# A top-k attention with a feed-forward behind it: the feed-forward's matmuls placed by the parity of the slot from the first block on

## The chip, the cores and the metric

The kernel runs on one core of one Trainium2 chip. The metric is the device time in microseconds (us); the kernel before took 1437.44 us as the median of three runs (1435.94 to 1437.99).

## The reference

Attention over 8 batches, 8 heads, 576 positions and a head size of 64, in float32. Each row of scores keeps its 32 largest values and drops the rest, then softmax, then the values. The result, 4608 tokens by 512, goes through a feed-forward whose activation is `h * cos(h)`:

```python
scores = scale * np.matmul(q, k.transpose(0, 1, 3, 2))
kth = np.partition(scores, -top_k, axis=-1)[..., -top_k:-top_k + 1]
scores = np.where(scores >= kth, scores, -1000000000.0)
attn = np.exp(scores - np.max(scores, axis=-1, keepdims=True))
attn = attn / (np.sum(attn, axis=-1, keepdims=True) + 1e-09)
x = np.matmul(attn, v).transpose(0, 2, 1, 3).reshape(B * S, H * D)
h = x @ w_in            # 512 -> 2048
out = (h * np.cos(h)) @ w_out   # 2048 -> 512
```

## The kernel before

**Units, slots, blocks.** A unit is 128 tokens for one pair of heads. There are 36 tiles of 128 tokens and 4 pairs, so 144 units, numbered 0 to 143. The main loop has one slot for each unit. In slot i, VectorE (DVE) searches the 32 largest scores of unit i (`topk_first`, `topk_round`), ScalarE (ACT) masks and exponentiates unit i-1 (`mask`, `exponentials`), GpSimd (POOL) splits unit i-2 into halves that go to DRAM and come back transposed (`split`, `write_halves`, `transposes`), and TensorE (PE) computes the scores of units ahead (`scores`) and, in even slots, the values of two units behind (`values`), which DVE scales into `xT` (`take_values`, L473). The four units of one tile make a block of the feed-forward. A tile that crosses from one batch to the next has two parts, so its matmuls are cut smaller.

**The search.** DVE folds each row of 576 scores into 288 maxima (`fold_high`, L260) and 288 minima. The minima come from POOL as sum minus maximum (`fold_sum` L276, `fold_low` L285), or, for the units in `BUSY` (7 to 10), from DVE (`fold_now`, L268).

**The feed-forward, in items.** PE's part of a block is 16 items: eight of `ff1` (256 of the 2048 hidden columns, L522), written here as a0 to a7, and eight of `ff2` (two of the 16 accumulation steps of the output, L597), written as B0, B2, ... B14 by their first step. Two items of `ff1` fill one PSUM bank. `take_first` (ACT, L536 and L538) empties the bank; after two banks the block has a tile of 1024 columns, on which POOL runs `reduce_first` (L558) and `reduce_second` (L567), ACT the sine (`sines`, L577) and POOL the product (`gate`, L584). After the last slot, `ff["end"]` moves the reductions and the gate to DVE. The feed-forward has two PSUM banks: one is held by the `ff2` of a block from its first item to its last, the other serves the `ff1` items two at a time.

**What sets the order.** The engines' orders are written out by hand: each engine executes its instructions in the order of the Python calls. `slot` (L696) calls `feed` three times: after round 2 of the search and before the scores and values, after round 3, and at its end. `feed(n)` places up to n items, taking turns between the two kinds (`kind`, `half`), as long as there is credit; credit grows by 5.0 in a slot less 0.9 for each unit scored there, up to 5.3 (L790). `can_first` asks that the block's `xT` is complete for two calls of `feed` and that a tile is free; `can_second` that the gate was placed at least `lag` calls ago (2, and 3 in the middle of the kernel, L627). After the last slot, `drain` runs three times and then `forward` until nothing is left, each placing two items.

**The weights.** Both matrices (w_in and w_out) arrive as 64-bit words in 32 chunks of 512 KB (`load_weights`) and are decoded during the first slots in three steps: ACT (`decode_first`, L133, L136), DVE (`decode_second`, L144), POOL (`decode_third`, L154). Twelve slots (`decoding`) are treated specially: there the sines and a gate come early in the slot (L710 to L712), and `ff["late"]` is false, so that reductions need not wait for the next slot.

Of the kernel before, what the change touches and what calls it, by code (L numbers as in the profile page):

```python
# [30 lines left out]
def kernel(  # L31
# [16 lines left out]
    NP = H // 2  # L48
# [43 lines left out]
        w_out.append(w)  # L92
        chunks.append((moe_w_out[f * P : (f + 1) * P, :], w))
    CHUNKS, XB = 7, 3
    BUSY = range(7, 11)
    ff = {"live": 0, "tick": 0, "now": 0, "credit": 0.0, "end": False, "kind": 0, "half": 0, "open": 0, "late": False}

    wq = {"next": 0, "loaded": deque(), "second": deque(), "third": deque(), "done": 0, "ready": 0}

    def staged(spare=0):  # L100
        return sum(c[2] == spare for k in ("loaded", "second", "third") for c in wq[k])
# [70 lines left out]
    NU = len(units)  # L172
# [81 lines left out]
    def fold_high(u):  # L254

        s, sc = u["s"], u["sc"]
        if u["n"] not in BUSY:
            del u["sc"]
# [13 lines left out]
    def fold_sum(u):  # L272

        s = u["s"].bitcast(I32)
        u["low"] = work.tile([P, 2, HS], F32, tag="low", name="low", bufs=1)
        nc.gpsimd.tensor_tensor(  # L276
            out=u["low"].bitcast(I32), in0=s[:, :, 0:HS], in1=s[:, :, HS:S], op=ALU.add
        )

    def fold_low(u):  # L280

        if u["n"] in BUSY:
            return
# [19 lines left out]
    def topk_first(u, w):  # L303

        u["top"] = tops[u["n"] % len(tops)]
        if w:
            merge_first(w)
        if u["n"] not in BUSY:
            fold_sum(u)
        fold_high(u)  # L310
        if w:
            merge_second(w)
        if u["n"] in BUSY:
            fold_now(u)
# [22 lines left out]
    def merge_first(u):  # L337
        n = TOPK // 2 + 1
        u["lesser"] = u["top"].rearrange("p j r i -> p j (r i)")[:, :, 2 * n : 3 * n]
        nc.vector.tensor_reduce(  # L340
            out=u["lesser"], in_=u["top"][:, :, 0:n], axis=mybir.AxisListType.X, op=ALU.min
        )
# [138 lines left out]
    for w in widths:  # L481
# [9 lines left out]
    first = deque((blk, i) for blk in blocks for i in range(2 * NF * blk["w"] // 512))  # L491
    second = deque(
        (blk, i, f) for blk in blocks for i in range(blk["w"] // P) for f in range(0, NF, 2)
    )
# [11 lines left out]
    def ff1(blk, i):  # L506
        w = blk["w"]
        nf = 256 // w
        part = i % 4
        if part == 0:  # L510
            blk["g"].append(ffw.tile([P, 1024], F32, tag="g", name="g", bufs=CHUNKS))
            blk["x"] = ffw.tile([P, 1024], F32, tag="x", name="x", bufs=XB)
            ff["live"] += 1
        if part % 2 == 0:
            open_bank()
            blk["mm"] = ps.tile([P, 512], F32, tag="mm", name="mm", bufs=2)
        g, mm = blk["g"][-1], blk["mm"]
        for a in range(nf):
            f = i * nf + a
            at = (part % 2 * nf + a) * w  # L520
            for c in range(NC):
                nc.tensor.matmul(  # L522
                    mm[:, at : at + w],
                    w_in[f // FC][:, c, (f % FC) * P : (f % FC + 1) * P],
                    blk["xT"][:, c],
                    start=c == 0,
                    stop=c == NC - 1,
                )
        if part % 2 == 0:
            return  # L530
        ff["open"] -= 1
        full.append((take_first, blk, g, blk["x"], mm, part // 2))
# [37 lines left out]
    def sines(least):  # L570

        n = sum(c[3] < ff["now"] for c in waiting)
        if n == 0 or (n < least and waiting[0][3] + 2 > ff["now"]):
            return
        for _ in range(n):
            blk, g, x, _ = waiting.popleft()
            nc.scalar.activation(out=x, in_=x, func=AF.Sin, bias=halfpi, scale=TWO_PI_BELOW)  # L577
            sined.append((blk, g, x))

    def gate(n):  # L580
        for _ in range(min(n, len(sined))):
            blk, g, x = sined.popleft()
            eng = nc.vector if ff["end"] else nc.gpsimd
            eng.tensor_tensor(out=g, in0=g, in1=x, op=ALU.mult)  # L584
            blk["gated"].append(ff["tick"])

    def ff2(blk, i, f0):
        w = blk["w"]
        if f0 == 0:
            open_bank()  # L590
            blk["o"] = ps.tile([P, 512], F32, tag="mm", name="o2", bufs=2)
        o = blk["o"]
        per = 1024 // w
        for f in range(f0, f0 + 2):
            g = blk["g"][f // per]
            at = (f % per) * w + i * P
            nc.tensor.matmul(  # L597
                o, g[:, at : at + P], w_out[f], start=f == 0, stop=f == NF - 1
            )
        if f0 + 2 < NF:  # L600
            return
        ff["open"] -= 1
        full.append((take_second, blk, i, o))
# [10 lines left out]
    def can_first():  # L614
        if not first:
            return False
        blk, i = first[0]
        if blk["left"] or ff["tick"] < blk["tick"] + 2 or wq["ready"] < (((i + 1) * (256 // blk["w"]) - 1) // FC + 1) * NC:
            return False
        return i % 4 > 0 or ff["live"] + staged() < CHUNKS  # L620

    def can_second():
        if not second:
            return False
        blk, i, f = second[0]

        lag = 3 if 3 * NP < ff["now"] < NU - NP else 2  # L627
        gated = sum(ff["tick"] >= t + lag for t in blk["gated"])
        return gated * 1024 // blk["w"] >= f + 2 and wq["ready"] >= NC * NF // FC + f + 2

    def feed(n):

        ff["tick"] += 1
        while n > 0 and ff["credit"] >= 1:
            kinds = (ff["kind"], 1 - ff["kind"])
            if ff["end"] and second and second[0][2] == 0:
                kinds = (0, 1)
            for kind in kinds:
                if (can_first, can_second)[kind]():
                    break  # L640
            else:
                return
            if kind == 0:
                ff1(*first.popleft())
            else:
                ff2(*second.popleft())
            if kind != ff["kind"] or ff["half"]:
                ff["kind"], ff["half"] = 1 - kind, 0
            else:
                ff["half"] = 1  # L650
            n, ff["credit"] = n - 1, ff["credit"] - 1

    scored, last, last_values = {}, {}, {}  # L660
    for i, u in enumerate(units):
# [13 lines left out]
    for n in range(NP, len(order)):  # L675
        i = last[order[n - 6]] if n >= 6 else 0
        load_at(max(i, 2 * NP + 2), load_qk, *order[n])
        i = last_values[order[n - 6]] if n >= 6 else 0
# [15 lines left out]
        transposes(x)  # L694

    def slot(i, u, w, x, z):  # L696
        n = (3, 4, 4, 3, 4, 3)[i] if i < NP + 2 else 2
        if i < NP:
            for load, b, hp in at_once[i]:
                load(b, hp)  # L700
        load_weights(n, nc.sync if i < NP + 2 else nc.scalar)
        if x:
            (turn if i < NP + 2 else send)(x)
        decoding = i < 3 * NP
        ff["late"] = False
        topk_first(u, w)
        fold_low(u)
        topk_round(u, 1)
        topk_round(u, 2)
        if decoding:  # L710
            sines(1)
            gate(1)  # L712
        decode_second(NP)
        decode_third()
        reduce_first()
        reduce_second()
        made = scored.get(i, [])
        if z:
            take_banks()
        feed(1)  # L720

        for m in made:
            scores(m)
        if z:
            values(z)


        if i % 2 and not decoding:
            sines(1)
        if w:  # L730
            mask(w)
        take_banks()
        if w:
            exponentials(w)
        if i + 1 < NU:
            take_scores(units[i + 1])
        topk_round(u, 3, both(w), z)
        ff["late"] = not decoding
        if i in at_slot:
            load, b, hp = at_slot[i]  # L740
            load(b, hp)
        gate(1)
        feed(1 if len(made) == 2 else 2)
        take_banks()
        decode_first(NP)
        reduce_first()
        reduce_second()
        feed(1 if len(made) == 2 else 3)

    def forward(n):  # L750
        ff["now"] += 1
        ff["credit"] = n
        take_banks()
        gate(2)
        reduce_first()
        reduce_second()
        sines(1)
        gate(2)
        feed(n)

    def drain(w, x, z):

# [24 lines left out]
    take_scores(units[0])  # L787
    decode_first(3)
    for i in range(NU):
        ff["credit"] = min(ff["credit"] + 5.0 - 0.9 * len(scored.get(i, [])), 5.3)  # L790
        ff["now"] += 1
        wq["ready"] = wq["done"]
        u, w, x = (units[i - n] if n <= i else None for n in range(3))
        z = units[i - 4 : i - 2] if i % 2 == 0 and i >= 4 else None
        if NP < i < NP + 3:
            z = units[2:4] if i == NP + 1 else None
        slot(i, u, w, x, z)
# [44 lines left out]
```

## Time and profile before

| | |
|---|---|
| median of 3 runs | 1437.44 us |
| the profiled execution: its own time | 1436.91 us |
| its span (first to last instruction) | 1435.1 us |
| PE busy | 1378.2 us, 96% |
| DVE busy | 1356.7 us, 95% |
| POOL, ACT busy | 1161.1 us, 1093.1 us |
| mean granted PE clock | 0.977 |

Times inside the profile are counted from the first instruction. Lines such as L597 are those of the listing above. "PEld" is PE's loading of weights, which overlaps its matmuls. The name of a group reads output <- inputs. Every matmul of the code appears as two in the trace, so an item of `ff1` is 16 of them and an item of `ff2` is 4.

### The profile page before, as it was taken

Reading aid. Unit: us, or ns where it says so; the run is one execution under the profiler, and the core shown is the slowest. Engines: PE = TensorE matmul, PEld = TensorE weight load, DVE = VectorE, ACT = ScalarE, POOL = GpSimd, SP = SyncE. Lnnn points to the kernel's source line nnn. Section 1 sums busy time; section 2 is a strip of 40 time slices with the busy share of each in tenths; the row PEclk is TensorE's granted clock in tenths of the full one; section 3 lists DMA queues with packets and bytes.
Section 4 is the critical chain, followed back from the end, with each engine's and each line's share of the span. In section 5 each row is a group of like instructions: output and inputs, shape, how many; then the busy total and the mean of one; then the engine's idle time right before and its main releaser. Section 6 shows DMA issues by size and latency. Waiting matters only on the chain.

```text
span 1435.1 us, 30310 instructions
## 1 busy us (share of the span) xinstructions
PE 1378.2 (96%) x10304; PEld 982.1 (68%) x10304; DVE 1356.7 (95%) x5236; ACT 1093.1 (76%) x1922; POOL 1161.1 (81%) x810
## 2 busy tenths in 40 slices
PE   5678899999999999999999999999999999999998
PEld 3455567777777767777777777777777777777765
DVE  8989999999999999999999999999999999999931
ACT  7877787787777787777778787777787778777742
POOL 5786888888888888888888898888888888888810
PEclk7698999999999999999999999999999999999999
DMA  9466676566655576557655557656755566655540
GB/s 306 175 183 176 191 202 182 142 172 190 180 161 152 152 190 185 162 147 202 181 158 151 155 170 196 179 140 178 192 173 155 155 159 165 172 147 146 153 100 15
DMA packets 427436, 240.01 MB, mean 167 GB/s; under 512 B 375952, under 2 KB 392592, under 8 KB 427280
## 3 DMA queue, kind: packets, MB, share of 16 engines
q1 hardware_dynamic: 420720, 224.22, 57.3%
q10 hardware_dynamic: 6560, 13.85, 2.7%
q8 instruction: 81, 1.33, 0.4%
q14 instruction: 75, 0.61, 0.1%
HBM read 45.09 MB, written 101.19 MB: 102 GB/s over the span
## 4 chain that ended last, share of the span: by engine, by line
PE 88%; DVE 10%; POOL 1%; ACT 1%; issue 0%; POOLq 0%; ACTq 0%
PE o L597 34%; PE mm L522 33%; PE rim L465 11%; PE sc L238 8%; DVE top L352 4%; DVE rest L357 3%; PE rim L238 2%; DVE low L357 1%; DVE rest L260 1%; DVE w_in L144 0%; POOL w_out L154 0%; POOL halves L412 0%; DVE w_out L144 0%; PE warm L782 0%; DVE xT L473 0%
## 5 line engine op out<-in xcount | busy, mean ns | idle before, releaser
L522 PEld LDWEIGHTS mm<-xT,w_in 128*128 128x128 f32 x4608 | 537.0, 192 | 72.2 <-issue 65.0
L597 PE MATMUL o<-w_out,g 128*128 128x512 f32 x1152 | 542.5, 606 | 18.3 <-POOL g L584 18.0
L522 PE MATMUL mm<-xT,w_in 128*128 128x128 f32 x4608 | 539.4, 276 | 4.6 <-DVE xT L473 3.0
L352 DVE MAX8 top<-rest 128x8 f32<-128x288 f32 x1152 | 478.8, 451 | 0.0
L412 POOL COPY halves<-s 128x2304 uint16<-128x2304 uint16 x140 | 294.6, 2104 | 151.4 <-ACT s L389 146.0
L357 DVE MATCH_REPLACE8 rest<-top,rest 128x288 f32<-128x288 f32 x864 | 376.4, 443 | 0.0
L597 PEld LDWEIGHTS o<-w_out,g 128*128 128x128 f32 x1152 | 205.3, 193 | 210.1 <-issue 190.5
L352 DVE MAX8 top<-low 128x8 f32<-128x288 f32 x576 | 241.7, 448 | 0.0
L389 ACT ACTIVATE s<-s,nd 128x576 f32<-128x576 f32 x288 | 220.1, 766 | 0.8
L285 POOL TENSOR_TENSOR low<-low,rest 128x576 int32<-128x576 int32 x140 | 197.7, 1412 | 11.0
L381 ACT ACTIVATE s<-s,top 128x576 f32<-128x576 f32 x288 | 206.1, 766 | 0.0
L276 POOL TENSOR_TENSOR low<-s 128x576 int32<-128x576 int32 x140 | 197.4, 1410 | 4.7 <-ACT s L252 4.7
L536 ACT ACTIVATE g<-mm 128x512 f32<-128x512 f32 x144 | 85.9, 597 | 140.7 <-PE mm L522 140.0
L567 POOL TENSOR_TENSOR x<-g,x 128x1024 f32<-128x1024 f32 x68 | 161.4, 2373 | 5.7
L584 POOL TENSOR_TENSOR g<-g,x 128x1024 f32<-128x1024 f32 x68 | 160.8, 2364 | 2.2 <-ACT x L577 2.2
L238 PE MATMUL sc<-k,q 64*128 64x448 f32 (+1 forms) x640 | 147.1, 580 | 6.2 <-DVE top L352 5.4
L465 PE MATMUL rim<-pT,v 128*64 128x128 f32 (+1 forms) x2560 | 146.2, 268 | 0.0
L465 PEld LDWEIGHTS rim<-pT,v 128*64 128x64 f32 x2560 | 128.3, 138 | 12.4 <-issue 11.1
L248 ACT COPY s<-sc 128x896 f32<-128x896 f32 x144 | 127.8, 888 | 3.2 <-PE sc L238 3.2
L252 ACT COPY s<-rim 128x256 f32<-128x256 f32 (+1 forms) x160 | 59.1, 369 | 90.3 <-PE rim L465 90.1
L357 DVE MATCH_REPLACE8 low<-top,low 128x288 f32<-128x288 f32 x288 | 125.4, 443 | 0.0
L260 DVE TENSOR_TENSOR rest<-sc,s 128x576 f32<-128x576 f32 x144 | 107.7, 748 | 6.4 <-ACT s L252 6.0
(55 smaller groups left out, 1210.9 us busy)
## 6 DMA issues: line engine op xcount, KB each, us to landing
rows<-halves SPq DMA_DIRECT2D x140, 640.0 KB, 3.0
out_dram<-ob ACTq DMA_DIRECT2D x36, 256.0 KB, 2.0
q<-in_q_dram SPq DMA_DIRECT2D x31, 288.0 KB, 3.4
st<-in_moe_w_in_dram SPq DMA_DIRECT2D x16, 512.0 KB, 6.8
v<-in_v_dram SPq DMA_DIRECT2D x32, 256.0 KB, 3.2
k<-in_k_dram SPq DMA_DIRECT2D x31, 144.0 KB, 3.3
k<-in_k_dram SPq DMA_DIRECT2D x32, 128.0 KB, 3.6
st<-in_moe_w_out_dram SPq DMA_DIRECT2D x8, 512.0 KB, 4.9
```

The costliest lines, as they stand in the source:

```text
L238: nc.tensor.matmul(to[r0 : r0 + rows, rim_bank(r0, j) if k0 else place(u["hp"], j), 0 : k1 - k0], st["q"][d, q0 : q0 + rows], st["k"][d, k ...
L276: nc.gpsimd.tensor_tensor(out=u["low"].bitcast(I32), in0=s[:, :, 0:HS], in1=s[:, :, HS:S], op=ALU.add)
L285: nc.gpsimd.tensor_tensor(out=low, in0=low, in1=u["rest"][:, :, HS:S].bitcast(I32), op=ALU.subtract)
L352: nc.vector.max(to[:, j], src[:, j])
L357: nc.vector.match_replace(rest[:, j], to[:, j], src[:, j], NEG)
L381: nc.scalar.activation(out=s[:, j], in_=s[:, j], func=AF.Prelu, bias=less[:, j, 1:2], scale=1.0, alpha=FAR)
L389: nc.scalar.activation(out=s[:, j], in_=s[:, j], func=AF.Exp, bias=nd[:, j : j + 1], scale=SCALE, accum_out=den[:, j, 0:1],)
L412: nc.gpsimd.tensor_copy(out=halves[:, :, 0 : 2 * S], in_=s.rearrange("p (k h) -> p h k", h=2))
L465: nc.tensor.matmul(room[i][d, r], lhsT, rhs, start=c == NT, stop=c == NT - 1)
L522: nc.tensor.matmul(mm[:, at : at + w], w_in[f // FC][:, c, (f % FC) * P : (f % FC + 1) * P], blk["xT"][:, c], start=c == 0, stop=c == NC - 1,)
L567: nc.gpsimd.tensor_tensor(out=x, in0=g, in1=x, op=ALU.subtract)
L597: nc.tensor.matmul(o, g[:, at : at + P], w_out[f], start=f == 0, stop=f == NF - 1)
```

## The change

`feed` no longer takes turns and counts no credit. It gets a list of kinds (0 for `ff1`, 1 for `ff2`) and places one item of each kind in the list if the gates allow it. Odd slots ask for a, then B B, then a a; even slots for B, then B, then a. `can_first` refuses before slot 6. The lag of 3 holds from the start, except near the end. `ff["late"]` is true in the decode slots as well, whose sines move to the place that they have later and whose early gate is dropped. Slot 3 loads four weight chunks and not three. `BUSY` loses unit 7. After the last slot, `feed_any` keeps the taking of turns, without credit, and the rule that a first `ff2` item lets `ff1` go ahead no longer asks for `ff["end"]`.

```diff
-    BUSY = range(7, 11)
+    BUSY = range(8, 11)
...
-        return i % 4 > 0 or ff["live"] + staged() < CHUNKS
+        return ff["now"] > NP + 2 and (i % 4 > 0 or ff["live"] + staged() < CHUNKS)
...
-        lag = 3 if 3 * NP < ff["now"] < NU - NP else 2
+        lag = 3 if ff["now"] < NU - NP else 2
...
-    def feed(n):
+    def item(kind):
+        if not (can_first, can_second)[kind]():
+            return False
+        if kind == 0:
+            ff1(*first.popleft())
+        else:
+            ff2(*second.popleft())
+        return True
+
+    def feed(*kinds):
 
         ff["tick"] += 1
-        while n > 0 and ff["credit"] >= 1:
+        for kind in kinds:
+            item(kind)
+
+    def feed_any(n):
+
+        ff["tick"] += 1
+        for _ in range(n):
             kinds = (ff["kind"], 1 - ff["kind"])
-            if ff["end"] and second and second[0][2] == 0:
+            if second and second[0][2] == 0:
                 kinds = (0, 1)
-            for kind in kinds:
-                if (can_first, can_second)[kind]():
-                    break
+            if item(kinds[0]):
+                kind = kinds[0]
+            elif item(kinds[1]):
+                kind = kinds[1]
             else:
                 return
-            if kind == 0:
-                ff1(*first.popleft())
-            else:
-                ff2(*second.popleft())
             if kind != ff["kind"] or ff["half"]:
                 ff["kind"], ff["half"] = 1 - kind, 0
             else:
                 ff["half"] = 1
-            n, ff["credit"] = n - 1, ff["credit"] - 1
...
-        n = (3, 4, 4, 3, 4, 3)[i] if i < NP + 2 else 2
+        n = (3, 4, 4, 4, 4, 3)[i] if i < NP + 2 else 2
...
-        if decoding:
-            sines(1)
-            gate(1)
...
-        feed(1)
+        feed(0 if i % 2 else 1)
...
-        if i % 2 and not decoding:
+        if i % 2 or decoding:
             sines(1)
...
-        ff["late"] = not decoding
+        ff["late"] = True
...
-        feed(1 if len(made) == 2 else 2)
+        feed(*((1, 1) if i % 2 else (1,)))
...
-        feed(1 if len(made) == 2 else 3)
+        feed(*((0, 0) if i % 2 else (0,)))
...
     def forward(n):
...
-        ff["credit"] = n
...
-        feed(n)
+        feed_any(n)
...
-        ff["credit"] = min(ff["credit"] + 5.0 - 0.9 * len(scored.get(i, [])), 5.3)
```

More of the change, by code (lines that the diff above doesn't have):

```diff
@@ L94 @@
     CHUNKS, XB = 7, 3
-    BUSY = range(7, 11)
-    ff = {"live": 0, "tick": 0, "now": 0, "credit": 0.0, "end": False, "kind": 0, "half": 0, "open": 0, "late": False}
+    BUSY = range(8, 11)
+    ff = {"live": 0, "tick": 0, "now": 0, "end": False, "kind": 0, "half": 0, "open": 0, "late": False}
     wq = {"next": 0, "loaded": deque(), "second": deque(), "third": deque(), "done": 0, "ready": 0}
```

## The prediction

> **What bounds the kernel now.** I read the page first: busy shares, slices, the chain that ended last.
>
> ```profile
> PE 1378.2 (96%) x10304; PEld 982.1 (68%) x10304; DVE 1356.7 (95%) x5236; ACT 1093.1 (76%) x1922; POOL 1161.1 (81%) x810
> ...
> PE   5678899999999999999999999999999999999998
> ...
> PEclk7698999999999999999999999999999999999999
> ...
> PE 88%; DVE 10%; POOL 1%; ACT 1%; issue 0%; POOLq 0%; ACTq 0%
> ```
>
> PE is idle for 57 us of the span, nearly all in the first six slices, where its clock is also cut. After that it is full. So the end comes at the moment from which PE runs without a gap, plus its remaining work, plus gaps at the end. The waits of the middle (230 to 1340 us) say the same: PE waits for nothing, and DVE only a little for the values that PE makes.
>
> ```profile
> DVE xT L473 <- ACT s L252: 11.8, 57, 0.6
> ```
>
> From the starts of the fold (L260), which opens a slot on DVE, two slots take 18.64 us when PE is full; where DVE sets the pace (slots 12 to 17) they take 18.38, an even one 9.39 and an odd one 8.99. PE's own sum for two slots is the same 18.64: four `ff1` items at 1.79, four `ff2` items at 1.72 to 1.82, scores 2.15, values 2.28. Then the timeline of the start, PE, DVE and POOL.
>
> ```profile
> 76.64 5.62 PE L522 MATMUL mm<-xT,w_in 128*128 128x128 f32 x48
> 88.74 6.34 PE L597 MATMUL o<-w_out,g 128*128 128x512 f32 x8 [6.47 <-POOL g L584]
> ...
> 112.35 8.19 PE L597 MATMUL o<-w_out,g 128*128 128x512 f32 x12 [7.63 <-POOL g L584]
> ...
> 151.54 3.26 PE L597 MATMUL o<-w_out,g 128*128 128x512 f32 x4 [3.93 <-POOL g L584]
> ```
> ```profile
> 85.96 3.01 DVE L144 TENSOR_SCALAR w_out<-w_out 128x512 int32<-128x512 int32 x2
> ...
> 105.18 0.49 DVE L473 TENSOR_TENSOR xT<-rim,pT 128x128 f32<-128x128 f32 x2 [3.62 <-ACT s L252]
> ```
> ```profile
> 86.17 2.51 POOL L584 TENSOR_TENSOR g<-g,x 128x1024 f32<-128x1024 f32 x1
> ```
>
> PE stands in front of an `ff2` item whose gate is still on POOL, three times, with scores and values queued behind it. The first time, DVE pays 3.62 us for it in slot 8. Each time PE then runs at half clock (eight matmuls in 6.34 us, against 3.44 later). And in slot 7 two decode steps of DVE take 3.01 us instead of 0.67, over the same stretch as POOL's gate.
>
> Last, the end, PE and ACT.
>
> ```profile
> 1363.70 1.88 PE L597 MATMUL o<-w_out,g 128*128 128x512 f32 x4
> 1365.42 1.95 PE L522 MATMUL mm<-xT,w_in 128*128 128x128 f32 x16
> 1367.21 3.60 PE L597 MATMUL o<-w_out,g 128*128 128x512 f32 x8
> 1370.64 1.95 PE L522 MATMUL mm<-xT,w_in 128*128 128x128 f32 x16
> 1373.85 2.05 PE L522 MATMUL mm<-xT,w_in 128*128 128x128 f32 x16 [1.26 <-ACT x L538]
> ```
> ```profile
> 1369.48 0.20 ACT L379 ACTIVATE nd<-nd 128x2 f32<-128x2 f32 x1 [1.46 <-DVE nd L372]
> ...
> 1371.68 0.76 ACT L389 ACTIVATE s<-s,nd 128x576 f32<-128x576 f32 x1
> 1372.34 0.19 ACT L389 ACTIVATION_READ_ACCUMULATOR s<-s,nd 128x1 f32 x1
> 1372.63 0.60 ACT L536 ACTIVATE g<-mm 128x512 f32<-128x512 f32 x1
> ```
>
> An `ff1` pair waits until ACT has emptied the bank of the pair before it, and that emptying stands behind the last unit's exponentials. Here it costs PE 1.26 us, because two `ff2` items (3.44 us) and a lone `ff1` cover the rest.
>
> [...] idle stretches of 6.5, 7.6 and 3.9 us are each followed by half clock, which ends 5.4, 5.6 and 4.0 us after work resumes; that costs 2.7, 2.8 and 1.7 us (half of the busy time in it). The 1.26 us gap has no such effect. [...] The two rows at 86 us agree (2.3 us lost), and slot 6 lost another 1.1 us the same way.
>
> **The change part by part.** The order in which the two built programs' instructions stand on each engine differs only before slot 14 and from slot 142 on; by the end of slot 13 both have placed 16 `ff1` and 8 `ff2` items. So the steady part costs the same, and only the two ends count.
>
> *Start, DVE.* Slot 4 decodes one chunk more: +0.34. In slot 7 the minima leave DVE (-0.66), and no gate runs on POOL beside the decode, but POOL's own minima (1.41 + 1.41 us after the halves) end about where the decode begins: I charge 0.4, bounds 0 and 1.1 (what slot 6 lost). Slot 7: 8.99 + 0.67 + 0.4 = 10.06 against 12.55, -2.5. In slot 8 only two `ff1` items, already runnable, stand ahead of the scores and values, so the 3.62 us go: -3.6. Sum up to slot 10: -5.8; its fold moves from 116.9 to 111.1 us. Slot 10 itself decodes one chunk fewer, -0.34. Slots 5 and 6 keep their DVE time: five PE items fewer are due there, and nothing waited on them. SP's only move is one weight load from ACT's queue into slot 3, ahead of all of the halves' transfers; ACT had gaps from 42 us on for the one decode more.
>
> *Start, PE.* The first `ff2` item now stands at the head of slot 10 and needs the gate of slot 9. On POOL that gate is behind the decode, which ended 9.65 us after the fold of slot 9 before (116.3 after 106.6) with the same two chunks; then 2.36 us of gate. Slot 9 is 10.3 us long, so the gate ends at 100.8 + 12.0 = 112.8. PE has been idle since about 104 and resumes at half clock: 2.5 us lost, the mean of the three cases (bounds 1.7 and 3.4). Scores and values of slot 10 stand behind it, so DVE waits nearly 2 us for `xT` there. From slot 10 on PE has the full load: slot 12 starts on PE at 112.85 + 18.64 + 2.5 = 134.0, DVE's fold near 132, the distance of the steady part (1.4 to 1.6 us). So PE is the bound from slot 10, not from slot 20. The next five pairs, with the cut tiles in them, cost 18.63, 18.43, 18.79, 19.07 (the same pairs around 510 to 570 us) after a first of 18.64: slot 22 starts at 227.6 against 230.3. **Gain 2.7 us**, where DVE alone offered 6. POOL has the load of the steady part plus at most two decodes (2.5 us); in slot 11 its gate is due at about 130.5 and needed at 134, so I cost it at nothing; without that slack its lateness adds one to one.
>
> *End.* The order becomes B0, scores, values, B2, a0 a1, B4 B6, a2 a3, a4 a5, values, with the credit's three early items gone. In the clock of the trace before: B2 from 1356.6, a0 and a1 to 1362.0, B4 and B6 to 1365.4, a2 and a3 to 1369.0. Now a4 needs the bank of a2 and a3, and its emptying stands on ACT behind the last exponentials. Those hang on DVE's distances of unit 143, 0.36 us earlier than before at best: emptying at 1372.3, a4 at 1373.5. PE stands for 4.5 us. Before, a pair began at 1373.85 with 3.44 us more of `ff2` done and the same `ff1`: 1373.5 + 3.44 - 1373.85 = **2.9 us lost** (the sum of gaps 4.5 - 1.26, less rounding). A gap of 4.5 us is longer than the 3.9 that halved the clock, so I add 1.7 us (bounds 0 and 2.8). Everything later on PE is the same work and covered by at least two items between each result and its use. **Loss 4.6 us.**
>
> *Sum.* 1436.9 (the profiled execution's own time) - 2.7 + 4.6 = 1438.8. It lies 0.5 under the median of the runs, so 1439.3 against 1437.44.
>
> **The rivals.** *The end keeps its full clock*: 1439.3 - 1.7 = 1437.6. [...] the 3.9 us case against.
> *DVE keeps the pace at the start*: if PE warms up quickly or the gate is early, the gain is up to 5 us: 1437.0. For it: DVE's stalls really go. Against: one gate at the head of slot 10.
> *The end doesn't stall*: if the exponentials are done before a3 ends, only the gain remains: 1434.7, and with the gain of the rival before 1432.4. Against it: ACT's order, and DVE's distances at 1369.3.
> *Slower: POOL is late for the gates of slots 9 and 11.* Its place is the head of slots 10 and 12, its price one us at the end for each us of lateness, since PE has no gap afterwards to win it back. From 1 us late the result is past the noise; with 3.5 us, what a reduction ahead of the gate costs (1.05 + 2.37), it is 1442.8. For it: decode and feed-forward now share slots 8 to 10 fully. Against: I find POOL free before each decode. That the change does nothing is excluded for the order, but not for the time.
>
> **How the numbers follow.** The forecast has 0.50, its own range 1437.3 to 1441.5; the end at full clock 0.15; DVE's pace 0.13; no stall at the end 0.09; POOL late 0.13. A measurement can tell about 0.2%, 2.9 us, from no change: 1434.6 and 1440.3. Slower: POOL late and three tenths of the forecast and a little of the rest, 0.31. Faster: the stall that isn't there, and some of DVE's pace, 0.13. Same: 0.56. The range 1434.6 to 1442.6 leaves out half of the outer two.
>
> **What would show it.** Right: PE's first `ff2` item near 113 us, at half clock, waiting for the gate; no 3.6 us of DVE in slot 8; decode in slot 7 near 1 us; PE at the head of slot 22 near 227.6; near the end one PE wait of 4 to 5 us for L538. Wrong: a wait for the gate later than slot 10, PE gaps between slots 11 and 20, or a4 behind a3 without a gap.

## The result, and the profile after

The changed kernel took 1439.58 us (median of 17 runs, 1438.36 to 1441.08), the kernel before 1437.16 us in the runs beside it. The ratio is 1.0019, with a 95% interval of 1.0011 to 1.0026: slower by 1.6 to 3.7 us. The difference of the medians, 2.4 us, lies under the 2.9 us (0.2%) that I had set as the bound of "no change"; the upper end of the interval lies above it. The forecast was 1439.3 us.

First the page of the changed kernel, with the same parts as before: busy times, slices, chain. (The profiled execution took 1440.46 us, its span is 1438.7 us.)

```profile
PE 1381.0 (96%) x10304; PEld 986.1 (69%) x10304; DVE 1354.9 (94%) x5235; ACT 1093.5 (76%) x1922; POOL 1166.2 (81%) x812
...
PE   5578999999999999999999999999999999999988
...
PEclk6679999999999999999999999999999999999999
...
PE 90%; DVE 5%; ACT 3%; DMA 1%; POOL 0%; SPq 0%; issue 0%; POOLq 0%
```

PE is full from the fifth slice on, where it was full from the sixth before, and DVE's share of the chain has halved: the bound has moved to PE early. The last two slices are thinner (8 and 8 against 9 and 8). So the page already suggests that something was won at the start and given back at the end. The stages give the sizes. I cut the execution at the starts of the fold (L260) that opens a slot on DVE, and at the end of PE's last matmul:

| stretch | before | after | difference |
|---|---|---|---|
| first instruction to the fold of slot 4 | 47.55 | 49.44 | +1.89 |
| slot 4 to slot 22 | 181.31 | 178.82 | -2.49 |
| slot 22 to slot 142 | 1121.03 | 1121.04 | 0.0 |
| slot 142 to PE's last matmul | 81.51 | 85.67 | +4.16 |

I don't put the first row down to the change: slots 0 to 2 hold the same instructions in both programs, slot 3 takes 10.33 us in every profile of this study, and the eleven other profiles lie between 47.3 and 48.3 us in this row. In this one execution the first fold starts 0.5 us later, and then DVE waits 1.3 us for a decode of ACT, whose weights come late. Without that row the change is -2.49 + 4.16 = +1.7 us, inside the interval.

The start, in the timelines of PE, DVE and POOL:

```profile
101.43 7.87 PE L522 MATMUL mm<-xT,w_in 128*128 128x128 f32 x64
115.49 3.78 PE L597 MATMUL o<-w_out,g 128*128 128x512 f32 x4 [6.18 <-POOL g L584]
```
```profile
87.22 1.28 DVE L144 TENSOR_SCALAR w_out<-w_out 128x512 int32<-128x512 int32 x2
...
101.95 0.49 DVE L473 TENSOR_TENSOR xT<-rim,pT 128x128 f32<-128x128 f32 x2 [0.86 <-ACT s L252]
...
124.26 0.49 DVE L473 TENSOR_TENSOR xT<-rim,pT 128x128 f32<-128x128 f32 x2 [1.57 <-ACT s L252]
```
```profile
110.58 2.54 POOL L154 TENSOR_TENSOR w_out<-w_out,st 128x512 int32<-128x512 int32 x2 [3.23 <-issue]
113.07 2.36 POOL L584 TENSOR_TENSOR g<-g,x 128x1024 f32<-128x1024 f32 x1
```

Of PE's three waits for a gate one is left, at the head of slot 10, where POOL's gate follows the decode without a gap. The item behind it runs at half clock (3.78 us for four matmuls, 1.98 later). The decode of slot 7 fell from 3.01 to 1.28 us, DVE's 3.62 us in slot 8 to 0.86. In slot 10 there is a new 1.57.

The end, PE and then ACT:

```profile
1357.82 3.73 PE L522 MATMUL mm<-xT,w_in 128*128 128x128 f32 x32
1361.39 3.60 PE L597 MATMUL o<-w_out,g 128*128 128x512 f32 x8
1364.82 3.73 PE L522 MATMUL mm<-xT,w_in 128*128 128x128 f32 x32
1372.56 5.26 PE L522 MATMUL mm<-xT,w_in 128*128 128x128 f32 x32 [4.00 <-ACT x L538]
```
```profile
1368.40 0.20 ACT L379 ACTIVATE nd<-nd 128x2 f32<-128x2 f32 x1 [2.43 <-DVE nd L372]
...
1370.60 0.76 ACT L389 ACTIVATE s<-s,nd 128x576 f32<-128x576 f32 x1
1371.27 0.19 ACT L389 ACTIVATION_READ_ACCUMULATOR s<-s,nd 128x1 f32 x1
1371.36 0.57 ACT L536 ACTIVATE g<-mm 128x512 f32<-128x512 f32 x1
1371.84 0.67 ACT L538 ACTIVATE x<-mm,quarter 128x512 int32<-128x512 f32 x1
```

Read the two side by side: PE ends a2 and a3 at 1368.6 and could begin a4 if its bank were empty. ACT has waited 2.43 us for DVE's distances, until 1368.4; it then executes the mask and the exponentials, and only then the two instructions that empty the bank. PE's 4.00 us end with the second of them, and its next pair takes 5.26 us where a pair takes 3.7.

### The profile page after: what moved, and what is told of

It is laid out like the page before. It is cut to its first block, busy times and chain, and to the rows that moved or that the text cites. A ratio compares the mean times of both kernels' runs of the same rounds, so it can differ in the third digit from the quotient of the medians.

```text
span 1438.7 us, 30312 instructions
## 1 busy us (share of the span) xinstructions
PE 1381.0 (96%) x10304; PEld 986.1 (69%) x10304; DVE 1354.9 (94%) x5235; ACT 1093.5 (76%) x1922; POOL 1166.2 (81%) x812
## 4 chain that ended last, share of the span: by engine, by line
PE 90%; DVE 5%; ACT 3%; DMA 1%; POOL 0%; SPq 0%; issue 0%; POOLq 0%
PE o L597 35%; PE mm L522 34%; PE rim L465 11%; PE sc L238 8%; DVE top L352 2%; PE rim L238 2%; DVE rest L357 1%; DMA st<-in_moe_w_in_dram 1%; ACT st L136 1%; ACT s L389 1%; ACT s L381 0%; ACT w_in L133 0%; DMA pT<-rows 0%; DVE low L357 0%; DVE rest L260 0%; DVE w_out L144 0%
## 5 line engine op out<-in xcount | busy, mean ns | idle before, releaser
L260 DVE TENSOR_TENSOR rest<-sc,s 128x576 f32<-128x576 f32 x144 | 107.7, 748 | 7.0 <-ACT s L252 6.5
```

## The experiments

Two theories stood against each other for the whole: mine (2.5 us won at the start, 4.2 lost at the end) and a rival (the start won nothing and holds the loss, the end is neutral). Times are medians of 5 to 21 runs (17 to 41 of the kernel before), each ratio is to the runs of the kernel before beside it (medians 1436.7 to 1437.3); the stretches, in us, are from each kernel's profile.

| run | time | ratio to before, interval | slot 4 to 22 | slot 142 to PE's end |
|---|---|---|---|---|
| before | 1437.2 | | 181.31 | 81.51 |
| after | 1439.58 | 1.0019, 1.0011 to 1.0026 | 178.82 | 85.67 |
| e1_start_only | 1435.30 | 0.9986, 0.9978 to 0.9994 | 178.90 | 81.51 |
| e2_end_only | 1441.64 | 1.0033, 1.0021 to 1.0046 | 181.48 | 85.87 |
| e3_bank_first | 1435.27 | 0.9987, 0.9981 to 0.9994 | 179.01 | 81.51 |
| e4_gate_first | 1437.16 | 1.0000, 0.9992 to 1.0008 | 175.92 | 86.79 |
| e5_both | 1432.32 | 0.9967, 0.9955 to 0.9980 | 177.04 | 81.50 |
| e6_spin_start | 1437.44 | 1.0003, 0.9995 to 1.0011 | 177.24 | 85.87 |
| e7_spin_end | 1437.43 | 1.0001, 0.9993 to 1.0009 | 178.89 | 84.25 |
| e8_minima | 1439.52 | 1.0016, 1.0009 to 1.0022 | 177.85 | 87.04 |
| e9_second_item | 1433.77 | 0.9978, 0.9970 to 0.9986 | 177.31 | 81.51 |
| e10_gate_late | 1442.04 | 1.0037, 1.0024 to 1.0051 | 180.42 | 87.06 |

A stretch comes from one execution, and slots with the same instructions differ between executions: slot 8 takes 10.7 to 12.0 us in the ten profiles that have the changed start, and slot 4 takes 11.5 us in e5 where it takes 10.7 in the others. So a difference of about 1 us in the fourth column is not by itself shown to be an edit's.

**e1_start_only: the change without its end.**

```diff
-        feed(*((1, 1) if i % 2 else (1,)))
+        feed(*((1, 0) if i == NU - 1 else (1, 1) if i % 2 or i == NU - 2 else (1,)))
...
-        feed(*((0, 0) if i % 2 else (0,)))
+        feed(*((1, 1) if i == NU - 1 else (0, 0) if i % 2 else (0,)))
```

> The changed kernel with the order of before in slots 142 and 143 and behind them (B0, B2 B4, a0, a1, B6 a2, B8 B10, then a3 a4), so only the change at the start is left. My theory (the start gains 2.5 us, the end loses 4.2): 1437.2 - 2.5 = 1434.7, PE's wait at the end back to 1.3 us and no half clock there. Rival (the start gains nothing, the loss lies there, the end is neutral): 1439.6.

Measured 1435.30 us, 1.9 us under before. The end takes 81.51 us, exactly as before, and PE's wait is 1.27 us again. The rival falls.

```profile
1372.12 2.05 PE L522 MATMUL mm<-xT,w_in 128*128 128x128 f32 x16 [1.27 <-ACT x L538]
```

**e2_end_only: the end of the change on the kernel before.** In slots 142 and 143 the three calls of `feed` take the lists of the changed kernel (`lists` places one item of each kind in turn, as the changed `feed` does):

```diff
-        feed(1)
+        lists(0 if i % 2 else 1) if i >= NU - 2 else feed(1)
...
-        feed(1 if len(made) == 2 else 2)
+        lists(*((1, 1) if i % 2 else (1,))) if i >= NU - 2 else feed(1 if len(made) == 2 else 2)
...
-        feed(1 if len(made) == 2 else 3)
+        lists(*((0, 0) if i % 2 else (0,))) if i >= NU - 2 else feed(1 if len(made) == 2 else 3)
```

> The kernel before with the order of the changed one in slots 142 and 143 and behind them, so only the change at the end is made. My theory: 1437.2 + 4.2 = 1441.4, with one PE wait of 4.0 us for the emptying of a bank and half clock behind it. Rival (the end is neutral): 1437.2.

Measured 1441.64 us, with 85.87 us for the end. The two halves of the change, -1.9 and +4.5 us, add up to +2.6; the change itself has +2.4, the same within the noise. The PE timeline of e2 shows the same wait:

```profile
1366.33 3.73 PE L522 MATMUL mm<-xT,w_in 128*128 128x128 f32 x32
1374.06 5.46 PE L522 MATMUL mm<-xT,w_in 128*128 128x128 f32 x32 [4.00 <-ACT x L538]
```

**e3_bank_first: who holds the bank.** In `drain`, ahead of the last unit's mask and exponentials:

```diff
         if x:
             send(x)
+        take_banks()
         if w:
             merge_first(w)
```

> The changed kernel, but after the last slot ACT empties the bank of a2 and a3 ahead of the mask and exponentials of the last unit. My theory (PE waits because the emptying stands behind them on ACT): the wait falls from 4.0 to about 1.3 us, too short for half clock, so 2.7 + 1.6 us are won: 1435.3. Rival (PE's wait comes from elsewhere, the last values or their transfer): 1439.6, and the later exponentials could cost up to 1.3 us more.

Measured 1435.27 us: PE's instructions and their order are those of the changed kernel, and 4.3 us are gone. ACT and PE of this kernel:

```profile
1366.84 0.60 ACT L536 ACTIVATE g<-mm 128x512 f32<-128x512 f32 x1 [2.61 <-PE mm L522]
1367.34 0.68 ACT L538 ACTIVATE x<-mm,quarter 128x512 int32<-128x512 f32 x1
1367.90 0.20 ACT L379 ACTIVATE nd<-nd 128x2 f32<-128x2 f32 x1
```
```profile
1368.07 3.84 PE L522 MATMUL mm<-xT,w_in 128*128 128x128 f32 x32 [1.26 <-ACT x L538]
```

The emptying fits into time in which ACT waited for DVE's distances anyway. So the wait came from ACT's order, not from the last values or their transfer.

**e4_gate_first: the gate of slot 9.** On POOL the gate goes ahead of the two decode steps of that slot:

```diff
         decode_second(NP)
-        decode_third()
+        if i != 2 * NP + 1:
+            decode_third()
...
         gate(1)
+        decode_third()
         feed(*((1, 1) if i % 2 else (1,)))
```

> The changed kernel, but in slot 9 POOL executes the gate ahead of the two decode steps, not behind them. My theory (the gate of slot 9 sets the start of PE's full load): the gate ends near 110 instead of 115.4, PE has hardly a gap before slot 10 and no half clock, its start moves up by over 5 us, and DVE takes over the pace until about slot 30: 4 to 5 us won, 1435.0. Rival (the first slots are set by DVE and by decode, not by the gate): within 0.5 us of 1439.6; or another wait of PE on POOL in slots 11 to 13 takes its place: 1 to 2 us won.

Measured 1437.16 us: 2.4 us won where I expected 4.5. POOL and PE of this kernel:

```profile
105.19 2.38 POOL L584 TENSOR_TENSOR g<-g,x 128x1024 f32<-128x1024 f32 x1
108.29 2.54 POOL L154 TENSOR_TENSOR w_out<-w_out,st 128x512 int32<-128x512 int32 x2 [0.72 <-DVE w_out L144]
```
```profile
107.62 1.98 PE L597 MATMUL o<-w_out,g 128*128 128x512 f32 x4 [0.77 <-POOL g L584]
...
113.03 1.57 PE L238 MATMUL sc<-k,q 64*128 64x448 f32 x4 [1.55 <-DVE low L268]
...
120.71 3.39 PE L522 MATMUL mm<-xT,w_in 128*128 128x128 f32 x28 [0.23 <-DVE xT L473]
```

The gate ends 6.4 us after the fold of slot 9 (at 101.18), not 12.0, and PE's first item starts at once. But then PE waits for DVE, in the scores of slot 10 and in the first item of block 1. My estimate had no term for these waits: PE can't run ahead of DVE there, since each block's first item needs the `xT` that DVE makes late in an even slot. In the profile the start won 2.9 us (178.82 to 175.92) and the end, whose order is that of the changed kernel, lost 1.1, which I put down to chance (see the last section).

**e5_both: e3 and e4 together.** Both edits, nothing else.

> The changed kernel with both edits: the gate of slot 9 ahead of the decode on POOL, and the bank of a2 and a3 emptied ahead of the last exponentials on ACT. If start and end are independent, as my theory has it, the gains add: 1439.6 - 4.5 - 4.3 = 1430.8, faster than both kernels. Rival (they share a bound, for instance DVE's pace at the end): 1433 or more.

Measured 1432.32 us, 4.9 us under before (0.9967, interval 0.9955 to 0.9980), the fastest kernel of the study. The gains of e3 and e4 are 4.3 and 2.4, together 6.7; it won 7.3 over the changed kernel, so they add within the noise. It falls 1.5 us short of the 1430.8, as e4 fell 2.1 us short of its own forecast.

**e6_spin_start and e7_spin_end: half clock alone.** Idle matmuls, whose result nobody reads, keep PE busy in the wait; e6 has only the six behind a7 at the start, e7 only the four behind a3 at the end:

```diff
+    def spin(n, tag):
+        shape = [P, 512] if tag == "mm" else [P, 2, 512]
+        t = ps.tile(shape, F32, tag=tag, name="spin", bufs=2)
+        to = t if tag == "mm" else t[:, 0]
+        for _ in range(n):
+            nc.tensor.matmul(to, ident, w_in[0][:, 0], start=True, stop=True)
...
+        if i == 2 * NP + 1:
+            spin(6, "mm")
...
+        if i == NU - 1:
+            spin(4, "sc")
```

> The changed kernel with six idle matmuls (identity by weights, 128x512, into a bank that is free, read by nobody) behind a7 in slot 9: 5.2 us of PE in the 6.2 us in which it waits for the gate. My theory (half clock after that wait costs 2.0 us): the first ff2 item and the scores of slot 10 run at full clock, PE is 2.0 us earlier from slot 12 on: 1437.6. Rival (the clock there is paid by nobody, since DVE has slack): 1439.6; if the idle matmuls delay the first item: 1440 or more.

Measured 1437.44 us, 2.1 us won by work that nobody needs. In its PE timeline the first item still waits for the gate, but at full clock:

```profile
107.55 5.42 PE L759 MATMUL spin<-w_in,ident 128*128 128x512 f32 x12 [0.33 <-ACT x L538]
113.81 1.98 PE L597 MATMUL o<-w_out,g 128*128 128x512 f32 x4 [0.84 <-POOL g L584]
115.72 1.02 PE L238 MATMUL sc<-k,q 64*128 64x448 f32 x4
```

> The changed kernel with four idle matmuls (identity by weights, into a free bank, read by nobody) between a3 and a4 near the end: 3.4 us of PE in the 4.0 us wait. My theory (the wait is followed by half clock that costs 1.6 us, the wait itself stays): a4 starts at the same place, all behind it at full clock: 1438.0. Rival (half clock there is hidden by other waits): 1439.6.

Measured 1437.43 us; its end takes 84.25 us against 85.67, so in the profiles half clock behind that wait costs 1.4 us and the wait itself the other 2.7 of the 4.16. By the medians (1439.58 and 1437.43) half clock costs 2.1 us; the last section shows how far one execution can differ. Both waits are paid twice: once as a gap, once as slow work behind it.

**e8_minima: unit 7's minima back on DVE.**

```diff
-    BUSY = range(8, 11)
+    BUSY = range(7, 11)
```

> The changed kernel with BUSY as before (7 to 10), so unit 7's minima are again on DVE. My theory: slot 7 costs DVE 0.66 us more and saves the contention of the decode with POOL's minima and a wait on them (0.6 + 0.6 us measured), so slot 7 is 10.1 against 10.2 us and the time is the same within 0.3 us of 1439.6. Rival (POOL is freed by 2.8 us and so its gate in slot 9 earlier): up to 2 us faster.

Measured 1439.52 us, no change. DVE's timeline has part of the trade: 0.66 us of visible minima more, the decode at 0.75 us instead of 1.28. But slot 7 took 10.58 us against 10.19, so 0.4 more and not 0.1 less: the wait for POOL's minima that I had counted as saved doesn't stand in slot 7 of the changed kernel. The rival falls too, since PE's first `ff2` item still starts 12.1 us after the fold of slot 9.

```profile
80.86 0.75 DVE L268 TENSOR_TENSOR low<-sc,s 128x576 f32<-128x576 f32 x1
...
86.38 0.75 DVE L144 TENSOR_SCALAR w_out<-w_out 128x512 int32<-128x512 int32 x2
```

**e9_second_item: the gaps of e4 filled.** On top of e5, B2 of block 0 moves in slot 10 from behind the values to behind B0:

```diff
-        feed(0 if i % 2 else 1)
+        feed(*((0,) if i % 2 else (1, 1) if i == 2 * NP + 2 else (1,)))
...
-        feed(*((1, 1) if i % 2 else (1,)))
+        feed(*((1, 1) if i % 2 else () if i == 2 * NP + 2 else (1,)))
```

> The kernel with both edits (gate of slot 9 ahead of the decode, bank emptied first), and in slot 10 the second ff2 item moved from behind the values to behind the first one. In the profile with the gate first, PE has gaps of 0.8, 0.4 and 1.6 us around the scores of slot 10, and half clock for 3.4 us behind them, which costs 1.7 us. My theory (those gaps and that clock are why the early gate gave 2.4 and not 4.5 us): the item fills the gaps, 1.8 us, and if the clock stays full another 1.7 us: 1429 to 1430.5. Rival (DVE or POOL holds slots 10 to 14): 1432.3, as with both edits.

Measured 1433.77 us, not faster than e5 but 1.4 us slower by the medians (2.0 us when each is taken against its own runs of before; the intervals overlap). My theory of the gaps falls:

```profile
118.18 0.71 PE L522 MATMUL mm<-xT,w_in 128*128 128x128 f32 x4
121.64 5.02 PE L522 MATMUL mm<-xT,w_in 128*128 128x128 f32 x28 [2.75 <-DVE xT L473]
```

The scores no longer wait, but a0 of block 1 now comes right behind the values and stands for DVE's `xT`; the gap has moved, and has half clock behind it (5.02 us for 28 matmuls, 3.39 in e4). In e5, slots 12 to 17 take 9.38 and 8.99 us in turn, which is DVE's own pace. So with the early gate DVE is the bound there, and that is what caps e4. A new order of PE's items should then have little left to win; only this one was run.

**e10_gate_late: the price of the gate.** Four idle multiplications on POOL ahead of the gate of slot 9:

```diff
+        for _ in range(4 if i == 2 * NP + 1 else 0):
+            nc.gpsimd.tensor_tensor(out=late, in0=late, in1=late, op=ALU.mult)
         gate(1)
```

> The changed kernel with four idle multiplications of 128x256 on POOL (a tile of their own, read by nobody) ahead of the gate of slot 9, about 2.4 us together. My theory (each us of lateness of that gate is a us at the end): 1442.0. Rival (there is slack between gate and bound): 1439.6 to 1440.5.

Measured 1442.04 us, 2.5 us more, for 2.69 us on POOL:

```profile
111.00 2.69 POOL L747 TENSOR_TENSOR late<-late 128x256 f32<-128x256 f32 x4
113.65 2.37 POOL L584 TENSOR_TENSOR g<-g,x 128x1024 f32<-128x1024 f32 x1
```

Later costs nearly one to one; earlier wins only down to DVE's pace, 2.4 us. In its profile slot 10 takes 14.27 us against 12.01, +2.3; slot 8 happens to be 0.5 us shorter, and the end has a second window of half clock, +1.4. So about 2.3 us of the 2.69 reach the pace of the slots; the agreement of the medians with "one to one" is partly luck.

## Why the prediction was right

The mechanism was right at both ends, and so was the sign of the sum. Point by point:

- **Only the ends differ.** Slots 22 to 142 took 1121.03 and 1121.04 us.
- **Start, DVE.** Slot 4 grew by 0.34 us, as worked out. Slot 7 took 10.19 us against 10.06 forecast: beside POOL's minima the two decode steps took 0.6 us longer (1.28 against 0.67), not 0.4. Slot 8 took 11.64, not 10.8: PE computes its values at half clock and for them waits 0.9 us for a transfer (lines below), so DVE still waits 0.86 there. I had taken that wait as gone, and I had no term for the half clock there: PE had just waited 5.2 and 4.1 us in the middle of its scores, until ACT and DVE had read earlier ones. e8, whose PE doesn't wait for the transfer, has 10.7 us in the same slot. Slot 6, which I had left as it was, became 0.33 us shorter.

```profile
97.20 0.69 PE L465 MATMUL rim<-pT,v_tail 64*64 64x128 f32 x4 [0.87 <-DMA pT<-rows]
97.82 3.68 PE L465 MATMUL rim<-pT,v 128*64 128x128 f32 x32
```

- **Start, PE.** The gate of slot 9 ended 12.0 us after the fold of slot 9, as forecast from the trace of before. PE's gap in front of it was 6.2 us; the prediction, with PE idle from about 104, implied nearly 9, because it had the `ff1` items end earlier. Half clock behind it lasted 4.0 us of work, 2.0 us lost against 2.5 forecast; e6 measured 2.1 by the medians and 1.6 in its profile. DVE waited 1.57 us in slot 10 ("nearly 2"). The gain was forecast as 2.7, and the profile has 2.49; e1 gives 1.9 by its median. That the sum is nearer than its parts is luck: the fold of slot 9 came 0.7 us later after that of slot 4 than forecast (53.97 against 53.25 us), and the half clock cost 0.5 us less.
- **End.** The wait was forecast as 4.5 us and was 4.00; half clock as 1.7, and e7 gives 1.4. Together 4.6 forecast, 4.16 in the profile, 4.5 by the median of e2. Counted from the fold of slot 142, the distances came 0.5 us earlier than before, where I allowed 0.36.
- **The rivals.** Full clock at the end didn't occur in any of the profiles with a wait of 4.0 us (after, e2, e4, e6, e8, e10). "DVE keeps the pace" is what the edit of e4 makes of the kernel, not the change itself. POOL was on time in slot 11 (gate until 132.9, needed at 136.1).

Two of the prediction's sums are off: 1373.5 + 3.44 - 1373.85 is 3.1 and not 2.9 us, and the mean of 2.7, 2.8 and 1.7 is 2.4 and not 2.5. Put right, they move the forecast by about 0.1 us, to 1439.4. The extra gap at the end, 4.00 - 1.26 in the traces, was 2.7 us.

Taken from the profiles, the errors in time are of both signs and under 0.6 us each, except slot 8; by the medians, the gain at the start was 0.8 us smaller than forecast.

## What to carry to other kernels

When a bound engine runs full for most of a kernel, a change of its order is worth what it does to the gaps at the two ends, and each gap has to be looked up where its release is queued: here one release stood behind a decode on POOL and one behind exponentials on ACT, and moving each ahead of that work (e5) turned a loss of 2.4 us into a gain of 4.9. Before moving work into a gap, ask which wait comes next for the items left behind: in e9 the gap only moved. In these profiles every stall of PE of 3.9 us or more had half-clock work behind it, so such a stall was paid twice, as the gap and as the slow work: 2.7 and 1.4 us at the end of the changed kernel, by the profiles of after and e7.

## What the runs showed of the hardware

- **Half clock behind the same stall differed from run to run.** After the same 4.00 us wait at the end, the half clock lasted one window of 3.4 us in after, e2 and e6 (end: 85.67 to 85.87 us) and two in e4, e8 and e10 (86.79 to 87.06). That is 1.2 us of scatter in the time, with the same program order behind it. A window is here the unit of the record: in the traces of before and after each stretch at one clock, from the first recorded one to the last change, is a whole multiple of 3.41 us (1 to 375 of them).
- **The clock went with how busy PE had been in the window before.** I cut the twelve traces, from 10 to 1410 us, into windows of 3.41 us at the recorded changes of the clock. The 58 full-clock windows ahead of half clock were busy for at most 0.57 of their time, those ahead of full clock for at least 0.44. From half clock, full clock came back only after windows that were busy for 0.87 or more (70 of 73); after the 177 below that it stayed half. The traces of before and after alone: at most 0.30 ahead of half clock (10 windows) and at least 0.54 ahead of full; back to full after 0.89 or more (12), still half after 0.82 or less (31). In the six cases at the end, the first half-clock window was busy for 0.89, 1.00 and 1.00 (after, e2, e6) and for 0.57, 0.73 and 0.74 (e4, e8, e10). So half clock also followed windows in which PE was busy for a part of the time, and the length of a gap, by which my prediction went, doesn't say all. An estimate from these figures and the 3.41 us: a gap of 4.0 us leaves a window with at most 0.41 wherever the windows lie, and a lone gap of 1.3 us leaves none under 0.62 (the 1.26 us gap before: 0.63, and the clock stayed full). By the same estimate a gap in between depends on its place: the 2.75 us in e9 fell into one window, and half clock followed.
- **DVE's decode and POOL's subtraction slowed each other, and it was the later one that took longer.** In slot 6 of the kernel before, POOL's subtraction came first and took 1.41 us, and DVE's three decode steps beside it took 2.10. In the changed kernel the decode steps came first and took 1.09, and the subtraction 2.31. Whichever started second took 1.0 us (decode) or 0.9 us (subtraction) more than where it came first; the median subtraction takes 1412 ns before and 1415 ns after. What lies behind it the traces don't show.

Before:

```profile
74.32 2.10 DVE L144 TENSOR_SCALAR w_out<-w_out 128x512 int32<-128x512 int32 x3
```
```profile
74.05 1.41 POOL L285 TENSOR_TENSOR low<-low,rest 128x576 int32<-128x576 int32 x1
```

After:

```profile
76.54 1.09 DVE L144 TENSOR_SCALAR w_out<-w_out 128x512 int32<-128x512 int32 x3
```
```profile
76.60 2.31 POOL L285 TENSOR_TENSOR low<-low,rest 128x576 int32<-128x576 int32 x1
```
